# Layer two of a fused attention and two-layer MLP kernel: one operand sum moved from a DMA to VectorE, one summing DMA queued later, and another pair of steps sharing its weight tiles

## The chip, the core and the metric

The kernel runs on one core of a Trainium2 chip. The time is the device time of one launch in microseconds (us). The kernel before took 1100.82 us as the median of three runs (1098.08 to 1101.04). All profiles here are of one execution on the chip. Names of engines: PE is TensorE, ACT is ScalarE, DVE is VectorE, POOL is GpSimd, SP is SyncE.

## The reference, cut to what matters

```python
def reference(q, k, v, tau, ...):              # N = 6016 tokens, C = 256, F1 = 1536, F2 = 2048
    x = attention(q, k, v, tau)                # column norms, softmax over a 256 x 256 score, v @ a
    x = rms_norm(x) * rms_g                    # layer one
    g = x @ w_gate
    x = (silu(g) * (x @ w_val)) @ w_out
    h = x @ w_in                               # layer two, 256 -> 2048 -> 256
    return (h - tanh(h)) @ w_out2
```

Everything is float32. The kernel splits each operand into a high and a low part and multiplies three times (high x high, low x high, high x low) with the faster matmul form, so one "product" below is three matmuls.

## The kernel before, in words

Tokens stand in columns. They are worked through in pairs of blocks of 512 columns (one pair has two blocks of 448). Layer two takes five full pairs and, last, the pair of 448.

In layer two a pair is worked in eight units (`j` = 0 to 7), each 256 of the 2048 hidden rows. Two blocks of hidden rows times two blocks of tokens make a 2 x 2 block product, and `unit` computes it with seven products instead of eight (PSUM banks X, T, Y, Z; the seven weights are S3, A11, A22, A12, S1, S2, S4). In each unit ACT copies bank X to bank Y (`Yh<-Xh`) before PE can go on with `Yh<-T2`; ACT copies T to `m5`; DVE adds Y and m5 into Z and into `s`. Then each of the four results goes through tanh on ACT and a subtraction on DVE: c11, c12, c22, c21.

The output matrix is applied in two ways. Units 6 and 7 use plain products (`second_unit`; weights from `out2_weight`; operands named `uc`). Units 0 to 5, called steps here, use seven products too (`second_seven`, class `Seven`): W11 takes c11, S1 takes c11 + c12, N3 takes c12 + c22, M2 takes c11 + c12 + c22; these four come in a first phase. After step 5 the four accumulator banks are copied away (`turn`, tiles `part`) and combined by four summing DMAs; in a second phase W12 takes c21, S4 takes c22, and W22 takes c11 + c12 + c22 + c21. Every operand is split into high and low by one ACT copy and one DVE subtraction (`split_form`), named by its product: `uW`/`ulW`, `uS`/`ulS`, `uN`/`ulN`, `uM`/`ulM`.

The operand sums are made by DMAs that add into SBUF (`add_by_dma`, L463). They are issued by POOL and follow one another in its queue. A step of before has four of them: c11 += c12, c12 += c22, c11 += c22, c11 += c21. In the trace a step's tiles have these names: step 0 c11 and c22 are `keepwraw`, c21 `keepvh`; step 1 c11 is `keepvh`, c22 and c21 `keepvraw`; step 2 c11 and c22 are `keepvl`, c21 `keeprr`; step 3 `keepwy`, `keepw12h`; step 4 `keepw12l`, `keepw11h`; step 5 `keepw11h`, `keepw11l`. c12 is always `wc`.

SBUF has no room for all output weights. Units 6 and 7 therefore take the place of weights that two steps need only in the first phase (W11, N3, M2, S1): `bring` copies in from DRAM the weights of unit 6 or 7 (`l26p`, `l27p`), and after that unit copies the step's own back (`l20p`, `l21p`). Before, the two steps are 0 and 1 (`SHARED` = 2), tiles `l20h`, `l20l`, `l21h`, `l21l` and two tiles that both print as `l2q`. Each turn is 512 KB per unit. SP issues these DMAs, the loads of the next pair (`y`), and the stores of the results (`outT`).

The order of all instructions is made before the build by a planner (`Graph.run` and `schedule`). It simulates the five queues with fixed costs; PE operations are ranked by a due key, and the output products get their key as "now plus a lag" (`LAG1`, `LAG2`, `LAG7`, `PHASE2`, in ns). Each engine then runs its list strictly in order. A summing DMA is planned to be done at `ADD_SETUP + ADD_TIME + ADD_SLACK` after its issue, and later if another one or an SP transfer is on the wire.

Of the kernel before, what the change touches and what calls it, by code (L numbers as in the profile page):

```python
# [39 lines left out]
PATIENT, HOLD, TOLERANCE = ("ACT", "DVE"), 900.0, 60.0  # L40
DMA_SETUP, DMA_RATE, DMA_TAIL, DMA_ISSUE = 1000, 390.0, 900, 450
DMA_SLACK = 2200
ADD_ISSUE, ADD_SETUP, ADD_TIME, ADD_SLACK = 900, 1440, 1560, 850
STALL, STALL_COST = 40.0, 300.0


# [273 lines left out]
BEHIND = 4  # L320
WARM = 6
MARGIN = 450.0
LAG0, LAG1, LAG2 = 4100.0, 11000.0, 9500.0
SEVEN2, SHARED = 6, 2
LAG7 = dict(W11=3500.0, S1=8750.0, N3=8000.0, M2=9500.0)
PHASE2 = dict(W12=(250.0, 3050.0), S4=(5250.0, 2500.0), W22=(4250.0, 7000.0))
SKEW = 2


# [1 line left out]
def attn_moe_kernel(  # L331
# [129 lines left out]
        return o  # L461

    def add_by_dma(out, in_):  # L463
        g.op("POOL", ADD_ISSUE, lambda: nc.gpsimd.dma_start(  # L464
            out=ap(out), in_=ap(in_), accum_op=ALU.add), [in_, out], [out])

    def prod(out, w, x, n, start, key=None):
# [832 lines left out]
    class Seven(Accumulate):  # L1300

        def __init__(self, forms, group, units, sizes, finish, lag, lag7, home, weight):
            super().__init__(weight, 2 * (units - group), sizes, finish, lag, home)
            self.forms, self.group, self.lag7 = forms, group, lag7
            self.started, self.rest = set(), []

        def at(self, t, m):
            if (t, m) not in self.o:
# [11 lines left out]
                f(at)  # L1320

        def turn(self):
            n = self.sizes[0]
            self.kept = {}
            for t, m in ((0, 0), (1, 0), (0, 1), (1, 1)):
                k = self.kept[t, m] = sq_tile(f"part{t}{m}")
                activation(k[:, :n], self.at(t, m), AF.Copy, n, **(
                    dict(scale=-1.0) if t != m else {}))
                del self.o[t, m]
            self.started = set()  # L1330
            for a, b in (((1, 1), (0, 0)), ((0, 1), (1, 1)), ((1, 1), (1, 0)), ((1, 0), (0, 1))):
                add_by_dma(self.kept[a][:, :n], self.kept[b][:, :n])

        SUMS = {(0, 0): ("add", (0, 0)), (1, 0): ("sub", (1, 1)), (0, 1): ("add", (0, 1)),
                (1, 1): ("sub", (1, 0))}
# [144 lines left out]
    def second_seven(j, x, n, A, keep):  # L1480

        T = dict(c11=keep[0], c12=ut(f"wc12{j}")[:, :n], c22=keep[1], c21=keep[2])
        T = {c: cols(t, n) for c, t in T.items()}

        def form(name, c, t, m):
            A.form(j, name, split_form(f"{name}{j}", T[c], n), t, m)

        def out(c):
            def f(src):
                t = T[c]  # L1490
                activation(t, src, AF.Tanh, n)
                tt("sub", t, src, t, n)
                if c == "c11":
                    form("W11", "c11", 0, 0)
                if c == "c12":
                    add_by_dma(T["c11"], T["c12"])
                    form("S1", "c11", 1, 0)
                if c == "c12":
                    add_by_dma(T["c12"], T["c22"])
                    add_by_dma(T["c11"], T["c22"])  # L1500
                    form("N3", "c12", 0, 1)
                    form("M2", "c11", 1, 1)
                if c == "c21":
                    add_by_dma(T["c11"], T["c21"])
            return f

        def out_sum(Y, m5):
            s = cs(f"s22_{j}")[:, :n]
            add(s, Y, m5, n)
            out("c22")(s)  # L1510

        unit(unit2[j], x, n, f"h{j}", out("c11"), out_sum, out("c12"), out("c21"))

        def second(name, c, t, m):
            return lambda key: A.form(j, name, split_form(f"{name}{j}", T[c], n), t, m, key)

        return dict(W12=second("W12", "c21", 0, 0), S4=second("S4", "c22", 1, 0),
                    W22=second("W22", "c11", 0, 1))
# [173 lines left out]

    forms7 = [{} for _ in range(SEVEN2)]
    plain = []
    split2 = {j: new_dram(f"l2{j}p", [P, 2, 2 * C]) for j in (*range(SHARED), *range(SEVEN2, NU2))}
    shared = {}

    def out_sums(j):
# [8 lines left out]
        for i, name in enumerate(("S4", "M2", "S1")):  # L1707
# [1 line left out]
                s.view(lambda t, x=x, i=i: t[:, (3 * x + i) * P:(3 * x + i + 1) * P],  # L1709
                       k if i == 0 else "one")  # L1710
                for x, k in enumerate("hl"))
        if j < SHARED:
            shared[j] = [(s.view(lambda t: t.rearrange("p (x n) -> p x n", x=2)[:, :, P:], "one"),
                          lambda a: a[:, :, C:], 2)]
            shared[j] += [(out2[j][x].view(lambda t: t[:, 3 * C:], "one"), lambda a, x=x: a[:, x, :C], 1)
# [10 lines left out]

    def out2_weight(f, m):
        k, i = f // 2 - SEVEN2, f % 2
        sums, h, l = (o.buf for o, _, _ in shared[k])
        if i == 0:  # L1730
            at = 3 * C + m * P
            return tuple(x.view(lambda t: t[:, at:at + P], "one") for x in (h, l))
        return tuple(sums.view(lambda t, x=x: t[:, (3 * x + 1 + m) * P:(3 * x + 2 + m) * P], "one")
                     for x in range(2))
# [32 lines left out]
    for p, after in zip(SECOND, [*SECOND[1:], None]):  # L1767
# [9 lines left out]
        for j in range(NU2):  # L1777
            if j < SEVEN2:
                second.append(second_seven(j, x, n, A, keep[3 * j:3 * j + 3]))
                if j < SHARED:  # L1780
                    bring(SEVEN2 + j, j)
                if j + 1 == SEVEN2:
                    A.turn()
                    A.rest = sorted(
                        (g.main + at + i * step, name, i, second[i][name])
                        for name, (at, step) in PHASE2.items() for i in range(SEVEN2))
# [2 lines left out]
                A.flush(float("inf"))  # L1789
            second_unit(j, x, n, A, (after, j) == (None, NU2 - 1))  # L1790
            if after is not None:
                bring(j - SEVEN2, j - SEVEN2)
        for _ in thread:
            pass

# [36 lines left out]
```

## Time and profile before

| what | value |
|---|---|
| median of three runs | 1100.82 us |
| the profiled execution | 1100.79 us, span 1099.0 us |
| PE busy | 1084.1 us (99%) |
| DVE busy | 928.5 us (84%) |
| ACT busy | 740.8 us (67%) |
| POOL busy (issuing DMAs) | 147.3 us (13%) |
| granted TensorE clock | 1.00 in nearly all slices, mean 0.999 |
| layer two | from about 620 us on |

Busy time of PE is the union of matmul intervals that overlap (a 512-column matmul is shown with some 385 ns while the next one starts earlier), so short stalls are better seen in how many matmuls start in a stretch than in the busy share. A gap in front of an instruction, and what ended it, stands in square brackets in the timeline.

### The profile page before, as it was taken

What the parts mean: (1) busy time and instruction counts of PE and PEld (TensorE: products, weight loads), DVE (VectorE), ACT (ScalarE), POOL (GpSimd) and SP (SyncE); (2) the same over time, 40 slices, a digit from 0 to 9 for tenths busy, and PEclk for the clock granted to TensorE, in tenths of its full rate; (3) what the DMA queues carried; (4) which work ended last, traced back from release to release, by engine and by line L of the source; (5) the groups of instructions that cost most, each with busy time, mean ns of one, the idle gap of its engine ahead of it and who ended that gap; (6) DMA issues with size and microseconds to landing.
All of it is one profiled execution on the core that took longest, in us unless ns stands there. A gap on an engine that the chain in (4) does not pass through costs nothing.

```text
span 1099.0 us, 14761 instructions
## 1 busy us (share of the span) xinstructions
PE 1084.1 (99%) x4836; PEld 898.7 (82%) x4836; DVE 928.5 (84%) x1638; ACT 740.8 (67%) x1338; POOL 147.3 (13%) x174
## 2 busy tenths in 40 slices
PE   9999999999999999999999999999999999999998
PEld 8889988888888888888888888878877878778897
DVE  6999897986888799688867989979978979878787
ACT  7686476565566656656665879669668668677675
POOL 0000000000000000000000043143142142152151
PEclk9999999999999999999999999999999999999999
DMA  9953121114212221322343396597586596595493
GB/s 353 379 195 112 59 72 39 59 39 136 68 47 62 93 86 54 105 87 68 112 135 92 112 216 126 119 183 128 129 171 128 129 169 129 126 167 102 119 176 81
DMA packets 83437, 136.33 MB, mean 124 GB/s; under 512 B 9632, under 2 KB 35104, under 8 KB 83360
## 3 DMA queue, kind: packets, MB, share of 16 engines
q1 hardware_dynamic: 58736, 91.87, 25.2%
q0 software_dynamic: 24192, 43.13, 23.2%
q8 instruction: 38, 0.62, 0.2%
q10 hardware_dynamic: 432, 0.38, 0.1%
q14 instruction: 39, 0.32, 0.1%
HBM read 66.72 MB, written 25.45 MB: 84 GB/s over the span
## 4 chain that ended last, share of the span: by engine, by line
PE 81%; DMA 7%; DVE 4%; issue 4%; ACT 2%; POOL 1%; SPq 0%; DVEq 0%; ACTq 0%; POOLq 0%
PE acc L474 32%; PE Yv L474 6%; PE Yh L474 6%; PE Yg L474 6%; PE Xg L474 4%; PE Xv L474 4%; PE Xh L474 4%; PE S L482 3%; PE v L474 2%; PE g L474 2%; PE Zv L474 2%; PE Zg L474 2%; PE Tg L474 2%; PE Tv L474 2%; PE Zh L474 2%
## 5 line engine op out<-in xcount | busy, mean ns | idle before, releaser
L432 ACT ACTIVATE uc<-tc 128x512 fp32r<-128x512 f32 x120 | 75.2, 631 | 84.1 <-PE acc L474 71.9
L464 POOL DMA_DIRECT2D keepwraw<-wc x6 | 5.4, 892 | 685.7 <-DVE ulW L451 685.7
L451 DVE TENSOR_TENSOR ulc<-tc,uc 128x512 fp32r<-128x512 f32 x120 | 81.5, 683 | 18.2 <-ACT uc L432 15.6
L447 DVE TENSOR_TENSOR Zh<-Yh,m5h 128x512 f32<-128x512 f32 (+1 forms) x48 | 32.9, 685 | 14.6 <-PE Yh L474 11.3
L474 PE MATMUL acc<-uS,l2q 128*128 128x512 f32 (+1 forms) x144 | 43.8, 386 | 0.0
L482 PE MATMUL S<-q,k 128*128 128x256 f32 x188 | 42.4, 385 | 0.8 <-DMA k<-k_in 0.8
L447 DVE TENSOR_TENSOR Zv<-Yv,m5v 128x512 f32<-128x512 f32 x30 | 20.9, 698 | 25.7 <-PE Yv L474 19.3
L482 PEld LDWEIGHTS S<-q,k 128*128 128x128 f32 x188 | 35.8, 193 | 6.1 <-issue 1.1
L432 ACT ACTIVATE uN<-wc 128x512 fp32r<-128x512 f32 (+1 forms) x36 | 22.4, 622 | 23.8 <-DMA wc<-keepw12h 9.4
L447 DVE TENSOR_TENSOR s<-Yh,m5h 128x512 f32<-128x512 f32 (+1 forms) x48 | 32.4, 674 | 5.5 <-PE Yh L474 4.8
L451 DVE TENSOR_TENSOR ulN<-wc,uN 128x512 fp32r<-128x512 f32 (+1 forms) x36 | 24.4, 678 | 14.7 <-ACT uN L432 13.7
L447 DVE TENSOR_TENSOR acc<-acc,sq 128x512 f32<-128x512 f32 (+1 forms) x46 | 29.4, 677 | 8.4 <-ACT sq L432 7.7
L474 PE MATMUL Yh<-T2h,l2s 128*128 128x512 f32 (+1 forms) x96 | 30.4, 398 | 5.8 <-ACT Yh L432 5.6
L432 ACT ACTIVATE Yh<-Xh 128x512 f32<-128x512 f32 (+1 forms) x48 | 27.6, 575 | 11.8 <-DVE wc L447 8.5
L432 ACT ACTIVATE wc<-Zh 128x512 f32<-128x512 f32 (+1 forms) x48 | 27.7, 577 | 11.5 <-PE Zh L474 11.5
L447 DVE TENSOR_TENSOR wc<-Zh,wc 128x512 f32<-128x512 f32 (+1 forms) x48 | 32.3, 673 | 2.9 <-ACT wc L432 2.9
L432 ACT ACTIVATE m5h<-Th 128x512 f32<-128x512 f32 (+1 forms) x48 | 28.1, 585 | 9.3 <-PE Th L474 8.6
L451 DVE TENSOR_TENSOR ulc<-wc,uc 128x512 fp32r<-128x512 f32 (+1 forms) x48 | 31.9, 674 | 1.8 <-ACT uc L432 1.2
L432 ACT ACTIVATE uc<-wc 128x512 fp32r<-128x512 f32 (+1 forms) x48 | 29.4, 620 | 4.2 <-PE acc L474 3.7
L432 ACT ACTIVATE Yg<-Xg 128x512 f32<-128x512 f32 x30 | 17.5, 583 | 20.6 <-PE Xg L474 9.0
L474 PEld LDWEIGHTS acc<-uS,l2q 128*128 128x128 f32 x144 | 27.0, 188 | 5.0
L474 PE MATMUL acc<-uc,w10l 128*128 128x512 f32 x80 | 31.1, 389 | 0.0
(1107 smaller groups left out, 3939.4 us busy)
## 6 DMA issues: line engine op xcount, KB each, us to landing
vraw<-vT_in SPq DMA_DIRECT2D x11, 512.0 KB, 4.2
y<-r SPq DMA_DIRECT2D x22, 256.0 KB, 2.7
part<-part POOLq DMA_DIRECT2D x20, 256.0 KB, 3.4
outT<-part SPq DMA_DIRECT2D x20, 256.0 KB, 4.4
q<-q_in SPq DMA_DIRECT2D x8, 512.0 KB, 9.7
k<-k_in SPq DMA_DIRECT2D x8, 512.0 KB, 9.7
raw<-w_in_in SPq DMA_DIRECT2D x8, 512.0 KB, 4.0
l<-y SPq DMA_DIRECT2D x16, 256.0 KB, 2.2
```

The lines of the kernel that those rows point to most:

```text
L432: nc.scalar.activation(out=ap(out), in_=ap(in_), func=func, **{x: ap(a) for x, a in kw.items()})
L447: return dve(lambda: f(out=ap(out), in0=ap(a), in1=ap(b)), n, 2, [a, b], [out])
L451: lambda: nc.vector.tensor_sub(out=ap(out), in0=ap(in_), in1=f32(ap(hi))), n, 2,
L464: g.op("POOL", ADD_ISSUE, lambda: nc.gpsimd.dma_start(out=ap(out), in_=ap(in_), accum_op=ALU.add), [in_, out], [out])
L474: nc.tensor.matmul(o, ap(a), ap(b), start=start and i == 0, stop=i == 2, skip_group_check=True)
L482: lambda: nc.tensor.matmul(ap(out), ap(a), ap(b), start=start, stop=stop, **kw),
```

## The change

Per step, c11 += c12 is a DVE addition now; the other three sums stay DMAs. The last of them, c11 += c21, is put on a list (`sums`) and issued behind the next step's c11 += c22 (`add_sums`, with an explicit order against it); what is left on the list goes out at `turn`. The tiles shared with units 6 and 7 are those of steps 4 and 5 instead of 0 and 1: the weights of units 6 and 7 are brought in after step 5 has been written down, and brought back after units 6 and 7. The lags, the start and step of the second-phase products, and the planner's `ADD_SLACK` have new values; these set the order alone.

```diff
-ADD_ISSUE, ADD_SETUP, ADD_TIME, ADD_SLACK = 900, 1440, 1560, 850
+ADD_ISSUE, ADD_SETUP, ADD_TIME, ADD_SLACK = 900, 1440, 1560, 1200
-LAG0, LAG1, LAG2 = 4100.0, 11000.0, 9500.0
+LAG0, LAG1, LAG2 = 4100.0, 9250.0, 7750.0
-LAG7 = dict(W11=3500.0, S1=8750.0, N3=8000.0, M2=9500.0)
-PHASE2 = dict(W12=(250.0, 3050.0), S4=(5250.0, 2500.0), W22=(4250.0, 7000.0))
+LAG7 = dict(W11=6250.0, S1=6000.0, N3=8000.0, M2=9750.0)
+PHASE2 = dict(W12=(250.0, 2300.0), S4=(4000.0, 2500.0), W22=(4500.0, 2250.0))
...
         def turn(self):
+            self.add_sums()
...
+        def add_sums(self, last=None):
+            for out, in_ in self.sums:
+                o = add_by_dma(out, in_)
+                if last is not None:
+                    o.preds.setdefault(last, None)
+            self.sums = []
...
                 if c == "c12":
-                    add_by_dma(T["c11"], T["c12"])
+                    add(T["c11"], T["c11"], T["c12"], n)
+                    add_by_dma(T["c12"], T["c22"])
                     form("S1", "c11", 1, 0)
-                if c == "c12":
-                    add_by_dma(T["c12"], T["c22"])
-                    add_by_dma(T["c11"], T["c22"])
+                    last = add_by_dma(T["c11"], T["c22"])
+                    A.add_sums(last)
                     form("N3", "c12", 0, 1)
                     form("M2", "c11", 1, 1)
                 if c == "c21":
-                    add_by_dma(T["c11"], T["c21"])
+                    A.sums.append((T["c11"], T["c21"]))
...
-        if j < SHARED:
+        if j >= SEVEN2 - SHARED:
...
             if j < SEVEN2:
                 second.append(second_seven(j, x, n, A, keep[3 * j:3 * j + 3]))
-                if j < SHARED:
-                    bring(SEVEN2 + j, j)
                 if j + 1 == SEVEN2:
                     A.turn()
+                    for k in range(SHARED):
+                        bring(SEVEN2 + k, SEVEN2 - SHARED + k)
...
             if after is not None:
-                bring(j - SEVEN2, j - SEVEN2)
+                bring(j - SHARED, j - SHARED)
```

On ACT, the first place is around step 4 of the third pair. In the order of before, `uS<-keepvl` is the S1 operand of step 2, `Yh<-Xh` the copy of step 4 that PE waits for, `uM` the M2 operand of step 1 and `uN<-wc` (second from the end) the N3 operand of step 2:

```order
L432 ACTIVATE wc_7956<-Zh_7922 128x512
L432 ACTIVATE keepw12h_7946<-Yh_7892 128x512
L432 ACTIVATE uS_7973<-keepvl_7851 128x512
L432 ACTIVATE Yh_7978<-Xh_7958 128x512
L432 ACTIVATE m5h_7987<-Th_7969 128x512
L432 ACTIVATE uM_7992<-keepvh_7673 128x512
L432 ACTIVATE keepw12l_8005<-Xh_7958 128x512
L432 ACTIVATE uN_8012<-wc_7871 128x512
L432 ACTIVATE uW_8019<-keepw12l_8005 128x512
```

The same place in the order of after, where `uN<-wc` is the N3 operand of step 2, `uM` the M2 operand of step 2 and `uS` the S1 operand of step 3:

```order
L432 ACTIVATE wc_7959<-Zh_7936 128x512
L432 ACTIVATE keepw12h_7964<-s_3_7953 128x512
L432 ACTIVATE uW_7967<-keepwy_7941 128x512
L432 ACTIVATE uN_7973<-wc_7892 128x512
L432 ACTIVATE keepw12h_7964<-Yh_7913 128x512
L432 ACTIVATE Yh_7987<-Xh_7977 128x512
L432 ACTIVATE uM_7994<-keepvl_7866 128x512
L432 ACTIVATE m5h_8000<-Th_7990 128x512
L432 ACTIVATE uS_8008<-keepwy_7941 128x512
```

The S1 operand no longer stands right ahead of the copy to Y, and each step of after repeats the same ten places.

On SP, the second place is the start of the fourth pair. Before, `part` are the results of the third pair, `l20`, `l21` and `l2q` the shared tiles, `l20p`, `l21p` the steps' own weights and `l26p`, `l27p` those of units 6 and 7:

```order
L458 DMA l2q_5648<-l21p 128x2x256
L458 DMA outT<-part_8295 128x512
L458 DMA outT<-part_8260 128x512
L458 DMA l21h<-l21p 128x256
L458 DMA l21l<-l21p 128x256
L458 DMA outT<-part_8158 128x512
L458 DMA outT<-part_8271 128x512
L458 DMA l20h<-l26p 128x256
L458 DMA l20l<-l26p 128x256
L458 DMA l2q_5575<-l26p 128x2x256
L458 DMA l21h<-l27p 128x256
L458 DMA l21l<-l27p 128x256
```

After, the same stores stand between the transfers that bring back the weights of steps 4 and 5, and then come the loads for units 6 and 7 of the fourth pair and the first load of the pair after the next one:

```order
L458 DMA l2q5_5982<-l25p_138 128x2x256
L458 DMA outT<-part11_8316 128x512
L458 DMA outT<-part10_8255 128x512
L458 DMA l25h_5999<-l25p_138 128x256
L458 DMA l25l_6024<-l25p_138 128x256
L458 DMA outT<-part00_8196 128x512
L458 DMA outT<-part01_8286 128x512
L458 DMA l24h_5836<-l26p_139 128x256
L458 DMA l24l_5849<-l26p_139 128x256
L458 DMA l2q4_5815<-l26p_139 128x2x256
L458 DMA y000_9054<-y0_94 128x384
```

The list is the same length, but the loads of `l26p` stand behind products of step 4 now and not behind products of step 0.

## Rows read from the trace of the kernel before

**Rows 1.** Stretches: length, busy (x instructions) of PE, PEld, DVE, ACT, POOL, clock, DMA.

```profile
200.00:600.00 400.00, 400.00 (x1762) 329.86 (x1761) 326.82 (x589) 244.44 (x435) 0.00 (x0) 1.00 0.26 82
625.47:704.31 78.84, 78.83 (x346) 64.36 (x345) 71.63 (x117) 62.06 (x115) 24.58 (x29) 1.00 0.73 150
704.31:784.49 80.18, 78.73 (x342) 63.33 (x342) 69.32 (x113) 58.87 (x109) 24.35 (x28) 1.00 0.71 145
784.49:866.20 81.71, 79.71 (x344) 63.57 (x343) 70.31 (x114) 59.19 (x109) 24.42 (x28) 1.00 0.69 142
866.20:946.83 80.63, 78.30 (x344) 63.93 (x343) 70.17 (x115) 59.00 (x109) 24.48 (x28) 1.00 0.69 140
946.83:1027.06 80.23, 78.62 (x343) 63.41 (x342) 65.69 (x106) 57.47 (x106) 24.44 (x28) 1.00 0.66 131
```

**Rows 2.** Waits of PE from 620 us on: total us, times, longest.

```profile
PE Yh L474 <- ACT Yh L432: 5.6, 8, 2.0
PE acc L474 <- ACT uN L432: 1.0, 2, 0.8
PE acc L474 <- ACT uM L432: 1.0, 1, 1.0
```

**Rows 3.** Timeline of the fourth pair: start, us, engine, instruction, idle before it.

```profile
882.63 1.52 POOL L464 DMA_DIRECT2D keepvl<-wc  x1
...
889.69 0.63 ACT L432 ACTIVATE uS<-keepvl 128x512 fp32r<-128x512 f32 x1 [1.60 <-DMA keepvl<-wc]
890.00 0.86 POOL L464 DMA_DIRECT2D wc<-keepvl  x1 [3.46 <-DMA keepvl<-wc]
890.22 0.58 ACT L432 ACTIVATE Yh<-Xh 128x512 f32<-128x512 f32 x1
890.35 0.69 DVE L451 TENSOR_TENSOR ulS<-keepvl,uS 128x512 fp32r<-128x512 f32 x1 [1.15 <-ACT uS L432]
...
890.85 0.50 PE L474 MATMUL Yh<-T2h,l2s 128*128 128x512 f32 x1 [2.00 <-ACT Yh L432]
```

**Rows 4.** Waits of ACT from 620 us on: total us, times, longest.

```profile
ACT uN L432 <- DMA wc<-keepw12h: 9.4, 6, 2.5
ACT uN L432 <- DMA wc<-keepvraw: 7.7, 4, 3.1
ACT uM L432 <- DMA keepwraw<-keepwraw: 5.6, 6, 1.9
ACT uS L432 <- DMA keepw11h<-wc: 4.1, 4, 1.8
ACT uS L432 <- DMA keepvl<-wc: 2.2, 2, 1.6
```

**Rows 5.** DMA issues, 882 to 883 us: KB each, us to landing.

```profile
keepvl<-wc POOLq DMA_DIRECT2D x1, 256.0 KB, 7.0
```

**Rows 6.** DMA issues, 997 to 1001 us.

```profile
keepw11h<-keepw11l POOLq DMA_DIRECT2D x1, 256.0 KB, 3.3
```

**Rows 7.** DMA issues, 868 to 880 us.

```profile
outT<-part SPq DMA_DIRECT2D x4, 256.0 KB, 4.6
...
keepvh<-wc POOLq DMA_DIRECT2D x1, 256.0 KB, 5.5
...
l20h<-l26p SPq DMA_DIRECT2D x1, 128.0 KB, 4.1
```

**Rows 8.** Timeline of DVE, three instructions that follow without a wait.

```profile
871.51 0.68 DVE L447 TENSOR_TENSOR part<-part,acc 128x512 f32<-128x512 f32 x1
872.11 0.68 DVE L447 TENSOR_TENSOR keepvraw<-Yh,keepvraw 128x512 f32<-128x512 f32 x1
872.71 0.68 DVE L451 TENSOR_TENSOR ulS<-keepwraw,uS 128x512 fp32r<-128x512 f32 x1
```

**Rows 9.** Costliest groups on the page: busy us, mean ns of one.

```profile
L451 DVE TENSOR_TENSOR ulc<-tc,uc 128x512 fp32r<-128x512 f32 x120 | 81.5, 683 | 18.2 <-ACT uc L432 15.6
```

**Rows 10.** Busy time of a stretch inside the first pair, columns as in rows 1.

```profile
650.00:700.00 50.00, 49.99 (x219) 40.66 (x218) 46.71 (x76) 41.66 (x77) 14.83 (x17) 1.00 0.70 136
```

More of the change, by code (lines that the diff above doesn't have):

```diff
@@ L463, in add_by_dma @@
     def add_by_dma(out, in_):
-        g.op("POOL", ADD_ISSUE, lambda: nc.gpsimd.dma_start(
+        return g.op("POOL", ADD_ISSUE, lambda: nc.gpsimd.dma_start(
             out=ap(out), in_=ap(in_), accum_op=ALU.add), [in_, out], [out])
@@ L1304, in __init__ @@
             self.forms, self.group, self.lag7 = forms, group, lag7
-            self.started, self.rest = set(), []
+            self.started, self.rest, self.sums = set(), [], []
         def at(self, t, m):
@@ L1694, in attn_moe_kernel @@
     plain = []
-    split2 = {j: new_dram(f"l2{j}p", [P, 2, 2 * C]) for j in (*range(SHARED), *range(SEVEN2, NU2))}
+    split2 = {j: new_dram(f"l2{j}p", [P, 2, 2 * C]) for j in range(SEVEN2 - SHARED, NU2)}
     shared = {}
@@ L1728, in out2_weight @@
         k, i = f // 2 - SEVEN2, f % 2
-        sums, h, l = (o.buf for o, _, _ in shared[k])
+        sums, h, l = (o.buf for o, _, _ in shared[SEVEN2 - SHARED + k])
         if i == 0:
```

## The prediction, made before the run

> **What bounds the kernel now.** I read the busy table first: PE 99%, the other engines far below. Since matmul intervals overlap in this trace, 99% does not mean that nothing is lost, so I next counted matmuls by stretch [rows 1]. In 200 to 600 us, in layer one, 1761 of them start in 400 us: 0.2271 us each, with no stall. A full pair of layer two has 8 units x 7 products x 3, plus 6 steps x 7 x 3, plus 2 units x 4 results x 2 x 3 = 342 matmuls, or 77.7 us at that pace. The five full pairs, cut at each pair's first summing DMA, take 78.84, 80.18, 81.71, 80.63 and 80.23 us: 1.1, 2.5, 4.0, 3.0 and 2.5 us too long, 13.2 us in all. The reader is to see that the DMA share in these rows is about 0.70 against 0.26 in layer one, and that the first pair, where DVE is densest, loses least (part of its 1.1 is work, since its stretch holds 2 to 4 matmuls more than the others).
>
> What PE waits for is in the waits: chiefly the copy of bank X to Y on ACT, 5.6 us in 8 waits, and then split operands that ACT makes [rows 2]. Such a gap understates the loss, since a matmul is shown some 0.16 us longer (0.39 against 0.23) than the spacing of starts; the counting above holds both. Why ACT is late is seen in the longest of the eight [rows 3]: ACT stands at `uS<-keepvl` until the DMA c11 += c12 of step 2 lands, 1.60 us; the copy to Y is the next in its queue, and PE has been idle 2.00 us when it comes. That DMA, issued at 882.63, took 7.0 us to land [rows 5]; one of the same size late in a pair took 3.3 [rows 6]. At the start of a pair four stores, the weights of step 1 going back and the weights of unit 6 coming in run beside the sums, and one such sum takes 5.5 us [rows 7]. So the bound is PE, and what is lost in layer two is ACT's queue held up by summing DMAs. ACT waits for them in three kinds of places: `uN`, `uM` and `uS` [rows 4].
>
> **The change part by part.** The matmuls stay the same in number and shape, so PE's floor stays, and only the excess can move: 13.2 us in the full pairs, and in the last pair about 1.2 (its one wait of 1.0 for `uM` [rows 2] and 0.2 for the spacing). Together 14.4 us; a gain beyond that is excluded.
>
> First sum on DVE. It takes 36 of 144 summing DMAs of layer two away, and ACT's waits at `uS` with them (4.1 and 2.2 us are the two largest [rows 4]); what follows in POOL's queue goes out one place, some 0.9 us, earlier. It adds 36 additions on DVE. Three DVE instructions in a row start 0.60 us apart although one is shown with 0.68 [rows 8]; so 36 x 0.60 = 21.6 us, 3.6 per pair. By the code DVE has 113 instructions of this size in a full pair now (48 in the units, 50 low parts, 4 results, 11 for the next pair's operands) and 119 then: 71.4 us of 77.7, or 92%. What hides it is that DVE was not the bound at 46.71 of 50 us, 93%, while PE was busy for 49.99 [rows 10]. If that cover is gone, the price is that of the slower rival below. Per step, ACT's new order gives the two remaining sums this much time: c12's difference, the c22 difference, two low parts, c21's and the sum are six DVE places, 3.6 us, before c12 += c22 may go; `uN` stands one step (33 matmuls, 7.5 us) and two ACT places (1.2 us) after c12's tanh. So 5.1 us are left for an add that lands in 3.3 us undisturbed [rows 6], and in 5.5 to 7.0 at a disturbed start [rows 5, 7]: nothing lost inside a pair, up to 1.9 us per pair at its start if the company stays as it is.
>
> Last sum behind the next step's. c11 += c21 is read in the second phase alone, so nobody waits for it. It now waits for `ulM` of its step, which is done by then, and behind it in POOL's queue stands only the next step's c12 += c22, one step later. I cost it at 0; from 0 to 0.9 us (one place) if it is late.
>
> Shared tiles of steps 4 and 5. Bringing in the weights of unit 6 used to wait for the N3 and M2 products of step 0, and so fell into the first 12 us of a pair, beside the stores [rows 7]. Now it waits for products of step 4 and falls behind step 5, where the four `part` sums run; in the new order 21 products, 63 matmuls or 14 us, lie between the last M2 of step 4 and the first product that reads the incoming weights, against 4 us that such a load takes [rows 7]. The weights that go back are not wanted for four steps, 30 us. What is late next is the rest: four stores and 512 KB going back still stand at the start of a pair. So the company there shrinks by the 1 MB for units 6 and 7, and by one sum in four. I cost the move at 0 and its gain as part of the excess.
>
> Lags, `PHASE2` and `ADD_SLACK`. They change the order of PE everywhere, layer one too, where PE is busy 400.00 of 400 us [rows 1]; nothing can be won there, and a stall of a few tenths lost: I take 0, with 0.5 us as the bad end. The second phase is pressed together: from unit 7 to step 1 of the next pair the new order has 63 DVE instructions to 174 matmuls, 37.8 us to 39.5, or 96%. That is above anything the rows show; 0 to 1 us per pair, and I take 0.3.
>
> How much of 14.4 us stays? The nearest rows are the first pair's. It has the same four sums, but no stores of an earlier pair and no weights going back at its start, and it loses 1.1 us or less. I take 0.4 for a pair's start and 0.3 for the second phase, 0.7 per pair, 4.2 in six. The sum: 14.4 - 4.2 = 10.2 us, and 1100.79 (the profiled execution, whose span is 1099.0) - 10.2 = 1090.6 us. That execution lies at the median of the runs, 1100.82, so the sum stands against the median too.
>
> A rule of the Trainium skill speaks against the first part: SBUF — State Buffer, Who interferes with whom, says that a VectorE instruction with both inputs in SBUF contends with a GpSimd instruction that reads SBUF, and whichever comes second is blocked to the end of the first. The added sums have both inputs in SBUF. If POOL's issuing counted as such, each of the 36 could cost DVE up to the 0.86 us of an issue, 31 us in all, and the kernel would be slower. In the trace a POOL issue runs from 890.00 to 890.86, and `ulS`, with both inputs in SBUF, starts beside it at 890.35 and takes 0.69 us as elsewhere [rows 3]; so by the row it costs nothing, and I go by the row.
>
> **The rivals.** (a) Only the waits at `uS` go, and those at `uN` and `uM`, still DMA sums, eat the rest. For it: the largest waits of ACT are those, 9.4 and 7.7 us [rows 4]. Against it: they come late because of the queue of four and the company, and both get smaller. Price: take the listed `uS` waits, 6.3 us of 29, as the share of 14.4 that goes: 3.1 us, so 1097.7 us.
>
> (b) No change: what the sums no longer hold up is held up by stores at a pair's start and by DVE in the second phase. 1.9 + 1 us per pair over six is 17.4 us, more than is lost now; at the mean of today's loss, 14.4 : 6 = 2.4 per pair, the time stays 1100.8.
>
> (c) Slower: DVE becomes the bound. If its instructions cannot be set 0.60 us apart, since each waits for a fresh result, and cost the 0.683 of one [rows 9], a pair takes 119 x 0.683 = 81.3 us; five of them 406.4 against 401.6, and the time is 1105.6 us. It decides from 77.7 : 119 = 0.653 us per instruction. For it: 92% in a strict order, with a step's chain ACT, DVE, DMA, ACT. Against it: DVE at 93% in [rows 10] and the spacing in [rows 8].
>
> (d) The change doesn't do what it says, that is, the new order puts `uN` or `uM` right ahead of the copy to Y. In the order of before it was `uS`; in the new order `uN` stands two places ahead and c21's tanh between. It ends as (a).
>
> **How the numbers follow.** The forecast, 1090.6 us, has 0.64, with its own range from 1086.5 (nearly all of 14.4 us goes) to 1094.8 (half of the pairs' excess stays). Between that and (a), 1094.8 to 1097.5, 0.16; (a) beyond that and (b) 0.12; (c) 0.08. A measurement of this kernel can tell about 0.3%, 3.3 us, from no change: below 1097.5 is faster, 0.80; up to 1104 the same, 0.12; above, 0.08. The range from 1086.5 to 1098 leaves out some 0.03 below and 0.17 above.
>
> **What would show it.** In the profile after: matmuls per pair still 342, and pairs of about 78.4 us; no wait of ACT at `uS` for a DMA; PE's waits for the copy to Y down from 5.6 to about 2 us; DVE with 36 more additions and a share near 87% of the span; the issue of 36 fewer DMAs on POOL. (a) would show `uN` and `uM` waits as long as now; (c) would show PE waiting for the addition into Z and ACT for DVE's differences in all steps, not at the starts alone. The forecast is wrong if pairs stay above 80 us, and the step that failed is then named by who holds ACT in front of the copy to Y.

## The result, and the profile after

The changed kernel takes 1085.61 us, the median of 4 runs (1085.30 to 1086.95); the kernel before, run beside it, 1100.93 (1098.08 to 1101.49). The ratio is 0.9868, with a 95% interval from 0.9849 to 0.9887: 15.3 us less. The forecast of 1090.6 us had the sign and the mechanism, but the time lies 0.9 us below the low end of the range. Medians and ratios, here and below, are over fast executions: a slow one of f1_two (3882.87 us) and one of f2_three (1206.79 us) are left out.

The busy table of the profile after, engine by engine, as busy time, share of the span and instructions:

```profile
span 1084.1 us, 14708 instructions
...
PE 1077.9 (99%) x4836; PEld 900.9 (83%) x4836; DVE 945.6 (87%) x1674; ACT 739.6 (68%) x1338; POOL 116.3 (11%) x138
```

VectorE's share is the 87% that was forecast, and PE's 99% still tells nothing. The stretches between the first summing DMAs of the pairs do; these rows answer to [rows 1], with the same columns:

```profile
200.00:600.00 400.00, 400.00 (x1759) 328.53 (x1758) 323.28 (x590) 242.95 (x434) 0.00 (x0) 1.00 0.25 79
626.20:704.02 77.82, 77.82 (x344) 63.97 (x343) 75.41 (x125) 62.85 (x117) 19.39 (x22) 1.00 0.62 132
704.02:781.82 77.80, 77.80 (x345) 64.27 (x344) 73.55 (x120) 59.34 (x110) 19.26 (x23) 1.00 0.61 129
781.82:858.92 77.10, 77.10 (x342) 63.85 (x341) 73.17 (x119) 58.48 (x110) 19.22 (x22) 1.00 0.61 130
858.92:936.59 77.67, 77.67 (x344) 64.23 (x343) 73.13 (x121) 59.15 (x110) 19.27 (x23) 1.00 0.59 125
936.59:1013.39 76.80, 76.80 (x344) 64.11 (x343) 69.23 (x114) 57.60 (x107) 19.27 (x23) 1.00 0.57 117
```

The five pairs take 77.4 us on average, against 80.3 before and a floor of 77.7: nothing is left to win in them. (The third stretch holds two matmuls fewer than a pair, and 34 matmuls of the fifth are already narrower ones of the last pair, hence the two under the floor.) In all of them PE is busy from end to end. All that PE waits for in the whole run, as total, times and longest (answers to [rows 2]):

```profile
PE nrm L482 <- DVE mean L529: 1.1, 1, 1.1
PE Yh L474 <- DVE Zh L447: 0.5, 1, 0.5
```

The first wait is at the very start of the span (1.1 us) and is in both kernels. Of layer two only the second is left, at 1022.9 us in the last pair. Among the waits of ACT from 610 us on, one kind alone is still for a transfer (answers to [rows 4]):

```profile
ACT uM L432 <- DMA keepwraw<-keepwraw: 3.4, 5, 1.3
```

So that losses can be compared between kernels, I counted them in each trace in one way: from 600 us on, the distance between the starts of successive matmuls, less the 0.227 us that 512 columns take at PE's pace (and less for narrower ones), summed where it is over 0.03 us. By this count layer two loses 15.6 us before and 1.2 us after, 14.4 us less. The count leaves out what is lost in distances under its limit. From the start of the same matmul at 602 us (the 2701st) to that of the last one, before takes 492.5 us and after 477.3, 15.2 us less. The spans differ by 14.9 us: at the 201st matmul after is 0.4 us ahead, and the rest of layer one takes it 0.7 us longer. In the first 50 us one wait of before is absent after:

```profile
PE S L482 <- DMA k<-k_in: 0.8, 1, 0.8
```

What the sums now look like inside a pair is seen in POOL's and ACT's timeline of the fourth (start, length, engine, instruction):

```profile
874.77 0.88 POOL L464 DMA_DIRECT2D wc<-keepvl  x1 [3.80 <-DVE keepvl L447]
...
876.58 0.87 POOL L464 DMA_DIRECT2D keepvl<-keepvl  x1 [0.92 <-DVE ulS L451]
...
878.98 0.62 ACT L432 ACTIVATE uN<-wc 128x512 fp32r<-128x512 f32 x1
...
880.66 0.62 ACT L432 ACTIVATE uM<-keepvl 128x512 fp32r<-128x512 f32 x1
```

`wc<-keepvl` is c12 += c22; it landed in 3.28 us, at 878.05, and ACT's split `uN` starts 0.93 us later without a wait. The other steps inside pairs look alike, some 7.4 us apart; in the five full pairs `uN` follows the landing by 0.8 to 1.3 us in 22 of 25 of them. At the start of a pair the sums have company; the issues from 855 to 875 us, with KB and us to landing (answers to [rows 5 to 7]):

```profile
outT<-part SPq DMA_DIRECT2D x4, 256.0 KB, 4.4
wc<-keepwraw POOLq DMA_DIRECT2D x1, 256.0 KB, 3.3
...
keepwraw<-keepwraw POOLq DMA_DIRECT2D x1, 256.0 KB, 5.5
wc<-keepvraw POOLq DMA_DIRECT2D x1, 256.0 KB, 3.3
```

The stores are still there, but c12 += c22 of step 0 (`wc<-keepwraw`) lands in 3.3 us, and in 3.3 to 3.6 in every pair; before, it took 4.1 to 5.1 in the pairs that follow another. Only c11 += c22 of step 0 lands late, and ACT waits 0.47 to 0.55 us for it in four pairs without any loss to PE. In the last pair ACT's wait is 1.34, and PE loses the 0.5 us shown above (0.8 by the spacing).

### The profile page after: what moved, and what is told of

It reads as the page before. It is cut to its first block, busy times and chain, and to the rows that moved or that the text cites. A ratio compares the mean times of both kernels' runs of the same rounds, so it can differ in the third digit from the quotient of the medians.

```text
span 1084.1 us, 14708 instructions
## 1 busy us (share of the span) xinstructions
PE 1077.9 (99%) x4836; PEld 900.9 (83%) x4836; DVE 945.6 (87%) x1674; ACT 739.6 (68%) x1338; POOL 116.3 (11%) x138
## 4 chain that ended last, share of the span: by engine, by line
PE 96%; ACT 2%; DVE 1%; DMA 0%; issue 0%; POOL 0%; DVEq 0%; ACTq 0%; POOLq 0%
PE acc L474 39%; PE Yh L474 9%; PE Xh L474 6%; PE Yv L474 6%; PE Yg L474 6%; PE Xg L474 4%; PE Xv L474 4%; PE S L482 4%; PE Zh L474 3%; PE Th L474 3%; PE v L474 2%; PE g L474 2%; PE Zg L474 2%; PE Zv L474 2%; PE Tg L474 2%; PE Tv L474 2%
## 5 line engine op out<-in xcount | busy, mean ns | idle before, releaser
L451 DVE TENSOR_TENSOR ulc<-tc,uc 128x512 fp32r<-128x512 f32 x120 | 80.3, 684 | 1.8 <-ACT uc L432 1.6
L464 POOL DMA_DIRECT2D wc<-keepwraw x6 | 5.4, 894 | 683.6 <-DVE keepwraw L447 624.9
L447 DVE TENSOR_TENSOR wc<-Zh,wc 128x512 f32<-128x512 f32 (+1 forms) x48 | 32.6, 679 | 12.8 <-ACT wc L432 12.3
L432 ACT ACTIVATE tc<-Zg 128x512 f32<-128x512 f32 x30 | 18.0, 599 | 31.2 <-PE Zg L474 27.7
L432 ACT ACTIVATE tc<-Xg 128x512 f32<-128x512 f32 x30 | 17.9, 597 | 21.8 <-PE Xg L474 21.6
L474 PE MATMUL acc<-uc,w11h 128*128 128x512 f32 x80 | 31.1, 389 | 0.0
L474 PE MATMUL acc<-ulc,w10h 128*128 128x512 f32 x80 | 31.1, 389 | 0.0
L474 PE MATMUL acc<-uc,w10h 128*128 128x512 f32 x80 | 31.1, 389 | 0.0
```

What stands on the lines that cost most here:

```text
L432: nc.scalar.activation(out=ap(out), in_=ap(in_), func=func, **{x: ap(a) for x, a in kw.items()})
L447: return dve(lambda: f(out=ap(out), in0=ap(a), in1=ap(b)), n, 2, [a, b], [out])
L451: lambda: nc.vector.tensor_sub(out=ap(out), in0=ap(in_), in1=f32(ap(hi))), n, 2,
L464: return g.op("POOL", ADD_ISSUE, lambda: nc.gpsimd.dma_start(out=ap(out), in_=ap(in_), accum_op=ALU.add), [in_, out], [out])
L474: nc.tensor.matmul(o, ap(a), ap(b), start=start and i == 0, stop=i == 2, skip_group_check=True)
```

## The experiments

The theory: ScalarE's queue stood behind a chain of landings, and VectorE's sum takes one landing out of it. Rival 1: the company of the transfers was the cause, whoever waits. Rival 2: the new order did it. All results in one table; "loss" is layer two's by the count above. The losses are those of the profiled executions; f1_two's is read from the trace of f1_again, the same kernel, and the profiled execution of e2_late is its slowest, 1104.48 us. In every kernel but the two with added small transfers the span less this loss is 1083 to 1086 us, so the loss accounts for the time to some 3 us.

| kernel | median us | ratio to before, 95% | loss, us |
|---|---|---|---|
| before | 1099.3 to 1101.1 | 1 | 15.6 |
| changed | 1085.61 | 0.9868 [0.9849, 0.9887] | 1.2 |
| a1_sum | 1091.47 | 0.9924 [0.9907, 0.9941] | 5.5 |
| a2_share | 1099.17 | 0.9984 [0.9972, 0.9996] | 13.7 |
| a3_numbers | 1109.38 | 1.0086 [1.0069, 1.0104] | 22.9 |
| a4_defer | 1105.12 | 1.0048 [1.0034, 1.0061] | 21.7 |
| b1_no_sum | 1100.39 | 0.9992 [0.9982, 1.0003] | 14.2 |
| b2_no_share | 1089.24 | 0.9892 [0.9876, 0.9908] | 3.0 |
| b3_old_numbers | 1091.21 | 0.9912 [0.9893, 0.9932] | 4.4 |
| b4_no_defer | 1088.26 | 0.9882 [0.9867, 0.9898] | 3.6 |
| d2_before_order_dve | 1090.19 | 0.9910 [0.9895, 0.9924] | 4.8 |
| d1_after_order_dma | 1149.21 | 1.0443 [1.0422, 1.0464] | 62.7 |
| e2_late | 1097.49 | 0.9988 [0.9971, 1.0005] | 12.3 |
| e3_late | 1151.68 | 1.0458 [1.0433, 1.0483] | 58.3 |
| f1_two | 1093.09 | 0.9934 [0.9916, 0.9953] | 10.3 (f1_again) |
| f2_three | 1108.87 | 1.0079 [1.0054, 1.0104] | 22.1 |

Not all of this loss is waiting. In six traces PE's granted clock falls in layer two from 1.00 to 0.50, the 1.2 GHz level, beside waits of PE of 0.8 to 6.2 us, and matmuls of 512 columns then start 0.43 us apart. The loss in these stretches is 1.6 us in a3_numbers, 3.0 in a4_defer, 4.7 in d1, 1.5 in e2_late, 9.3 in e3_late and 1.7 in f1_again. The traces of the other kernels have no such stretch while matmuls run, so the comparisons of before, after, a1_sum, a2_share, b1 to b4, d2 and f2_three do not rest on it. Two stretches of e3_late, columns as above:

```profile
822.00:825.00 3.00, 3.00 (x15) 2.45 (x14) 2.84 (x5) 1.64 (x3) 1.79 (x2) 1.00 1.07 113
829.50:832.50 3.00, 3.00 (x8) 2.32 (x8) 2.44 (x5) 1.66 (x3) 1.28 (x2) 0.50 0.30 52
```

### One part at a time, added to the kernel before

a1_sum:

```diff
-                    add_by_dma(T["c11"], T["c12"])
+                    add(T["c11"], T["c11"], T["c12"], n)
```

> The kernel before with one part of the change: c11+=c12 of each step runs on VectorE, all else as before (the order is planned anew around it). Theory (ScalarE's queue stood behind the landing of this sum, its wait at uS): the uS waits for a transfer go, and with them most of the loss that VectorE's one sum can reach, 7 to 11 of the 15.3 us: 1090 to 1094 us. Rival 1 (the transfers themselves are slow when five sums follow each other, whoever waits; the deferral and the move of the stores cure that): 1097 to 1101 us, the waits only move to uN and uM. Rival 2 (the new lags and slack set the order and do nearly all of it): within 2 us of before.

1091.47 us, as the theory had it: 9 us of the gain. No wait at `uS` for a transfer is left. The longest that remain are those of `uN` and `uM` of step 1 on the two other sums, 3.8 and 3.6 us in all.

a2_share (the sharing steps are 4 and 5; the weights come back behind step 5):

```diff
-        if j < SHARED:
+        if j >= SEVEN2 - SHARED:
...
-                if j < SHARED:
-                    bring(SEVEN2 + j, j)
                 if j + 1 == SEVEN2:
                     A.turn()
+                    for k in range(SHARED):
+                        bring(SEVEN2 + k, SEVEN2 - SHARED + k)
```

> The kernel before with one part of the change: the two steps that share tiles with units 6 and 7 are steps 4 and 5, so that their weights are brought back later; sums, lags and slack as before. Theory: the stores of units 0 and 1 leave the first two steps of a pair, sums there land sooner, but ScalarE still waits at uS: 0 to 2 us less, 1099 to 1101 us. Rival 1 (company of transfers is the cause): 5 us less or more, 1096 us or under.

1099.17 us, 1 to 2 us less: rival 1 falls as far as these transfers go, for less company alone changes little.

a3_numbers:

```diff
-LAG0, LAG1, LAG2 = 4100.0, 11000.0, 9500.0
+LAG0, LAG1, LAG2 = 4100.0, 9250.0, 7750.0
```

(and with it `ADD_SLACK`, `LAG7` and `PHASE2` as in the change)

> The kernel before with one part of the change: the new lags of the second layer's work (LAG1, LAG2, LAG7, PHASE2) and ADD_SLACK 1200 instead of 850; every sum still a transfer. Theory: the planner leaves more time between a sum and its split, which cuts some of the waits at uM and uN but pushes work together elsewhere: 1097 to 1102 us. Rival 2 (the numbers do nearly all of it): 1086 to 1090 us.

1109.38 us, 9 us slower than before, and worse than either expected. Rival 2 falls as far as it says that the numbers do it alone: with the sums still in line as transfers, the new numbers only add loss.

a4_defer:

```diff
-                    add_by_dma(T["c11"], T["c22"])
+                    last = add_by_dma(T["c11"], T["c22"])
+                    A.add_sums(last)
...
-                    add_by_dma(T["c11"], T["c21"])
+                    A.sums.append((T["c11"], T["c21"]))
```

> The kernel before with one part of the change: c11+=c21 of a step is issued behind the next step's sums. Theory: nobody waits for this sum within its step, and the next step's first sum starts without its company; the wait at uS shrinks by some tenths of a us in five of six steps but stays: 1 to 4 us less, 1097 to 1100 us. Rival 1 (company of transfers is the cause): 1090 to 1095 us.

1105.12 us: slower than before by 5 us, a miss for both. PE's waits of layer two in this trace are of the old kind and longer than before (5.6 in [rows 2]), and 3.0 of the 21.7 us of loss are the lower clock behind the longest of them:

```profile
PE Yh L474 <- ACT Yh L432: 6.5, 7, 2.7
```

### One part at a time, taken from the changed kernel

b1_no_sum:

```diff
-                    add(T["c11"], T["c11"], T["c12"], n)
+                    add_by_dma(T["c11"], T["c12"])
```

> The changed kernel without one of its parts: c11+=c12 is a transfer again, the rest (deferral, sharing with steps 4 and 5, new numbers) stays. Theory (ScalarE behind the landing of this sum): waits at uS for a transfer come back, 6 to 11 us of the gain are lost: 1092 to 1097 us. Rival 1 (company of transfers): 0 to 3 us lost, 1086 to 1089 us. Rival 2 (the numbers): within 1 us of the changed kernel.

1100.39 us: all of the gain is gone, more than the theory had. ACT's waits at `uS` for this sum are back, the two largest of its waits for transfers being

```profile
ACT uS L432 <- DMA keepwraw<-wc: 8.9, 5, 2.4
ACT uM L432 <- DMA keepwraw<-keepwraw: 5.4, 4, 2.2
```

So the three other parts together are worth nothing without the sum (ratio 0.9992), though with it they are worth 5.9 us (a1_sum to the changed kernel).

b2_no_share:

```diff
-        if j >= SEVEN2 - SHARED:
+        if j < SHARED:
```

(and the weights brought back at steps 0 and 1, as before)

> The changed kernel without one of its parts: steps 0 and 1 share their tiles with units 6 and 7 again, whose weights are brought back there. Theory: c12+=c22 lands later in the first two steps of a pair (5 to 7 us instead of 3.3 to 3.5), over the 5.1 us that a step has for it; this is where the 0.4 us per pair were expected that the changed kernel does not show: 1086.5 to 1089 us. Rival: within 0.5 us of the changed kernel, since the sum on VectorE left room enough.

1089.24 us, 3.6 more than the changed kernel. Not by the expected way: at the pair starts c12 += c22 of step 0 lands in 3.1 to 3.7 us, not in 5 to 7. In the fourth pair c11 += c22 is late and ACT waits 1.06 us for it, where the changed kernel's wait is 0.47, and PE loses 0.8 us there. The rest of the loss lies scattered in small pieces. The ratio's interval overlaps that of the changed kernel.

b3_old_numbers:

```diff
-LAG0, LAG1, LAG2 = 4100.0, 9250.0, 7750.0
+LAG0, LAG1, LAG2 = 4100.0, 11000.0, 9500.0
```

(and the three others back too)

> The changed kernel without one of its parts: the lags and the slack of the kernel before. Theory: each step's splits come due earlier than their sums land in some steps, and the second phase is less even: 1086.5 to 1090 us. Rival 2 (the numbers do nearly all of it): 1096 to 1101 us.

1091.21 us, just above the expected stretch. Waits of ACT for sums, and of PE for the copy to Y behind them, come back in some steps:

```profile
PE Yh L474 <- ACT Yh L432: 1.3, 2, 0.9
```

b4_no_defer:

```diff
-                    last = add_by_dma(T["c11"], T["c22"])
-                    A.add_sums(last)
+                    add_by_dma(T["c11"], T["c22"])
...
-                    A.sums.append((T["c11"], T["c21"]))
+                    add_by_dma(T["c11"], T["c21"])
```

> The changed kernel without one of its parts: c11+=c21 follows at once in its own step. Theory: it lies ahead of no split of its own step, and meets the next step's c12+=c22 only at its end: 1085.5 to 1088 us. Rival 1 (company of transfers): 1090 to 1095 us.

1088.26 us, 2.7 more; here too the ratios' intervals overlap, so the worth of this part and of the sharing is the least certain. Most of its loss lies in the last pair and the second phase behind it, where c11 += c22 of step 0 takes 6.2 us to land and ACT waits 2.5 us for it.

In all eight kernels the order is planned anew, so they show what a part is worth with its own order, not the part alone. The small differences of b2 to b4 lie in layer two only in part by the count (1.9, 3.3 and 2.4 us more than after); between the same two matmuls as above the three take 3.5, 3.6 and 2.6 us more. Of b3's remainder 1.1 us lies behind the last matmul.

### The sum alone, with the order held

d2_before_order_dve (planned as before, another instruction issued):

```diff
-                    add_by_dma(T["c11"], T["c12"])
+                    g.op("POOL", ADD_ISSUE, lambda: nc.vector.tensor_add(
+                        out=ap(T["c11"]), in0=ap(T["c11"]), in1=ap(T["c12"])),
+                        [T["c12"], T["c11"]], [T["c11"]])
```

> The kernel before in its own order, but the instruction issued in the place of each transfer c11+=c12 is VectorE's addition. Theory (ScalarE behind a chain of transfers): this alone shortens the chain by a landing (3.3 to 7.0 us instead of 0.6), the waits at uS for a transfer go, those at uN and uM shrink, PE's excess in layer two falls from 15.6 to 3 to 8 us: 1088 to 1094 us. Rival (the order that is planned around the part does it): less than 4 us gained, 1097 to 1101 us.

1090.19 us. In the very order of before (apart from the 36 instructions the traces have the same lists on all engines), replacing 36 transfers by additions takes 10.9 of the 15.6 us away. PE's wait for the copy to Y falls from 5.6 us in 8 waits to one, while ACT still waits for the two other sums:

```profile
PE Yh L474 <- ACT Yh L432: 0.8, 1, 0.8
```

```profile
ACT uN L432 <- DMA wc<-keepw12h: 5.7, 5, 1.7
ACT uM L432 <- DMA keepwraw<-keepwraw: 3.5, 5, 1.4
```

The line itself is seen in POOL's waits. Before, c12 += c22 is held up by the landing of c11 += c12 in 25 of the 36 steps, 57 us in all; the largest row is

```profile
POOL wc L464 <- DMA keepvh<-wc: 17.5, 5, 5.7
```

In d2 POOL has no such wait, and ACT's waits for transfers fall from 8.3 to 0 us at `uS`, from 22.6 to 7.0 at `uN` and from 8.4 to 4.7 at `uM`. It was not less company that did it: c12 += c22 lands no sooner in d2 (median 4.3 us) than before (4.1). So rival 1 falls here too, and rival 2 with the order.

d1_after_order_dma (planned as the changed kernel, a transfer issued):

```diff
-                    add(T["c11"], T["c11"], T["c12"], n)
+                    dve(lambda: nc.gpsimd.dma_start(out=ap(T["c11"]), in_=ap(T["c12"]), accum_op=ALU.add),
+                        n, 2, [T["c11"], T["c12"]], [T["c11"]])
```

> The changed kernel in its own order, but c11+=c12 is a transfer issued from GpSimd in the place of VectorE's addition. Theory: c12+=c22 must wait until it has read c12, so a step has two landings in a row where there is room for one: some 3.6 us (0.9 issue and 3.3 landing less 0.6) later against 0.9 us between landing and uN, so up to 2.7 us in each of 36 steps, less what ScalarE has of room: 1110 to 1180 us. Rival (room is ample in the new order): within 8 us of the changed kernel, 1086 to 1094 us.

1149.21 us, 64 more than the changed kernel, 1.8 per step: its order has no room for a second landing in line. ACT waits at `uS` in 32 of the 36 steps. The late split holds VectorE at `ulS` in all 36 (63.0 us), and PE waits for `s` behind it, 43.5 us in 35 waits; 4.7 us of the loss are the lower clock. The largest line of ACT:

```profile
ACT uS L432 <- DMA keepvh<-wc: 18.3, 6, 3.5
```

### How much room a landing has

e2_late, and e3_late with LATE = 3:

```diff
+    LATE = 2
+    tiny = [dram.tile([P, 2], F32, tag=f"late{i}", name=f"late{i}") for i in range(LATE + 1)]
+    def late_add(out, in_):
+        def emit():
+            for i in range(LATE):
+                nc.gpsimd.dma_start(out=tiny[i], in_=mean32.t)
+            nc.gpsimd.dma_start(out=ap(out), in_=ap(in_), accum_op=ALU.add)
...
-                    add_by_dma(T["c12"], T["c22"])
+                    late_add(T["c12"], T["c22"])
```

> The changed kernel, its order kept, with two transfers of 1 KB issued on GpSimd ahead of each c12+=c22: it and c11+=c22 go out and land some 1.7 us later (two issues of 0.86), c12+=c22 about 5.0 us after it could go. By the prediction's room of 5.1 us: nothing is lost, 1085 to 1088 us. By the room seen in the trace of the changed kernel (uN starts 0.93 us behind the landing, 4.2 us in all) and no further room on ScalarE: 0.8 us in each of 36 steps, 28 us, 1114 us.

> The same with three such transfers: c12+=c22 lands about 5.9 us after it could go. By the prediction's room of 5.1 us: 0.8 us in each of 36 steps, 28 us, 1114 us. By a room of 4.2 us: 1.7 us in each, 60 us, 1146 us. If ScalarE's own room behind the wait covers it (the changed kernel waits up to 1.3 us at uM and PE loses nothing): under 5 us, below 1091 us.

1097.49 us (from 1095.53 to 1104.48) and 1151.68 us. Against the changed kernel, 6 and 9 us of the two profiled spans are lost ahead of layer two: in the first 20 us PE waits 3.3 and 5.6 us for `k`, and the granted clock is 0.50 for part of the time. Why stays open. Both expectations rest on a delay that did not happen. The small transfers have no data to wait for, so POOL issues them right behind the sums of the step before, long ahead of their own sum. At the start of the third pair of e2_late:

```profile
792.78 0.88 POOL L464 DMA_DIRECT2D keepwraw<-keepwraw  x1 [0.66 <-DVE ulS L451]
793.36 1.44 POOL L473 DMA_DIRECT2D late<-mean  x2
799.52 0.90 POOL L474 DMA_DIRECT2D wc<-keepvraw  x1 [4.72 <-DVE keepvh L447]
```

They act as company. From 790 to 800 us in e2_late:

```profile
keepwraw<-keepwraw POOLq DMA_DIRECT2D x1, 256.0 KB, 6.8
...
late<-mean POOLq DMA_DIRECT2D x2, 1.0 KB, 7.9
```

That is still a dose. In the changed kernel and these two, whose planned order is one, a wait of ACT for a sum can be set beside PE's loss (spacing) from 3 us before its end to 6 us after. At `uM` at the pair starts, waits of 0.46 to 0.55 us cost nothing in five cases, 1.8 to 2.0 us cost 0.8 to 0.9, and 2.3 cost 1.1: ACT has 0.5 to 1.2 us to spare there. At `uN` inside pairs it has less. Waits of 0.64 and 1.96 us cost 0.26 and 1.58, and in e3_late two of 3.0 cost 2.8 and 4.3, the latter with 1.6 us of lower clock in it: 0.2 to 0.4 us to spare in these four, at most 0.8 in the others, beside the 0.93 us by which `uN` follows an undisturbed landing. So c12 += c22 has 3.3 + 0.9 + 0.2 to 0.8, which makes 4.4 to 5.0 us in all. The prediction's 5.1 us is a little too much, and it had put all of it ahead of `uN`, where the trace has 4.2. Why three small transfers hurt inside pairs where two do little (c12 += c22 lands in 4.3 to 7.7 us in four steps between 743 and 776 us of e3_late) stays open.

### How far VectorE carries

f1_two, and f2_three with the second line too:

```diff
-                    add_by_dma(T["c12"], T["c22"])
+                    add(T["c12"], T["c12"], T["c22"], n)
...
-                    last = add_by_dma(T["c11"], T["c22"])
-                    A.add_sums(last)
+                    add(T["c11"], T["c11"], T["c22"], n)
+                    A.add_sums()
```

> The changed kernel with c12+=c22 on VectorE as well (the order is planned anew): 125 VectorE instructions of 512 columns in a full pair, 75.0 us of 77.4 at 0.60 us each. Theory: the uN wait is gone for good and VectorE, at 97%, still keeps up for most of the pair: 1085 to 1092 us. Rival (VectorE becomes the bound, at 0.653 us per instruction or more): 125 x 0.653 = 81.6 us per pair, 4.2 x 6 = 25 us more, 1110 us or over.

> The changed kernel with c12+=c22 and c11+=c22 on VectorE: 131 instructions in a full pair, 78.6 us at 0.60 us each against PE's 77.4. Theory: VectorE is the bound by 1.2 us per pair and PE starts to wait for its results: 7 us more at least, 1092 to 1100 us. Rival (0.653 us per instruction): 85.5 us per pair, 49 us more, 1134 us. If below 1089 us, VectorE's instructions can be set closer than 0.60 us apart.

> f1_two once more, for its profile: 1093 us. Theory (VectorE at its limit): full pairs of 78.4 to 79.2 us, VectorE without idle time in the steps, TensorE waiting for VectorE's results (Zh, s), ScalarE for no sum. Rival (landings): ScalarE waits at uM for c11+=c22 by 0.9 us and more in most steps and TensorE waits for the copy to Y.

f1_two took 1093.09 us, 7.5 more than the changed kernel, f1_again 1096.27. Its trace agrees with neither side whole. PE's one kind of wait in layer two is for VectorE; but ACT's only waits for a transfer are five at pair starts and one of 0.2 us, and the longest of these, 3.6 us for a sum that took 8.0 us to land, stands beside 4.6 of the 10.3 us lost, 1.7 of them in the lower clock:

```profile
PE Yh L474 <- DVE Zh L447: 3.7, 3, 2.7
```

```profile
ACT uM L432 <- DMA keepwraw<-keepwraw: 7.8, 5, 3.6
```

f2_three took 1108.87 us, 23 more than the changed kernel, three times what 0.60 us per place allows for. Two of its pairs, columns as above:

```profile
718.63:800.74 82.11, 79.45 (x341) 62.87 (x340) 81.10 (x133) 60.63 (x109) 8.67 (x11) 1.00 0.35 85
800.74:881.88 81.14, 79.40 (x343) 63.57 (x343) 80.30 (x132) 60.38 (x109) 8.66 (x10) 1.00 0.36 85
```

VectorE is busy 99% of them, and its instructions start 0.62 us apart on average, not 0.60. Its timeline shows longer places:

```profile
724.51 0.69 DVE L447 TENSOR_TENSOR keepvl<-s,keepvl 128x512 f32<-128x512 f32 x1
725.11 0.69 DVE L447 TENSOR_TENSOR keepvl<-keepvl,wc 128x512 f32<-128x512 f32 x1
725.84 0.69 DVE L447 TENSOR_TENSOR wc<-wc,keepvl 128x512 f32<-128x512 f32 x1
726.56 0.69 DVE L451 TENSOR_TENSOR ulS<-keepvl,uS 128x512 fp32r<-128x512 f32 x1
```

The third instruction, c12 += c22, follows the second by 0.73 us instead of 0.60: it overwrites c12, which the second still reads, and starts as that one ends. The fourth starts as ACT's `uS` ends. Over four pairs the places are 12.1 us longer than 0.60 each; 2.4 us of this lie in front of c12 += c22, 3.8 in front of the addition into Z (`Zh`), and 3.0 in front of `ulS` and `ulN`, which need ACT's split. PE then waits for `Zh` 20 times, 12.0 us in all. Here VectorE is the bound, its places drawn out by what stands between its own and ACT's instructions.

## Why the prediction was wrong, point by point

- The bound: right. PE's floor stayed (the five pairs average 77.4 us against 77.7), and layer two's excess moved. The cause was right too: with the order held, taking the landing of c11 += c12 out of ACT's queue is worth 10.9 us of loss (d2), and putting it in costs 64 us (d1).
- The ceiling, "14.4 us; a gain beyond that is excluded": mis-sized. By spacing the loss before was 15.6 us, 13.7 in the five pairs and 2.0 in the last one (13.2 and 1.2 were taken), and the profiled execution of before held a 0.8 us wait for k at its start besides.
- **The step that failed**: how much of the excess stays, "0.4 for a pair's start and 0.3 for the second phase, 0.7 per pair, 4.2 in six". The trace after has 1.2 us in all, 0.2 per pair. Of the 5.0 us between forecast and median this term is 3.0, the ceiling 1.2, what the count does not hold 0.5, and 0.3 is between executions.
- Why it failed: deferral, shared tiles and lags were costed at 0, one by one. The forecast is, to within 1 us, what the sum alone gives (1090.19 and 1091.47 us), and d2's remaining loss of 4.8 us is close to the 4.2 that were kept. That closeness is luck: the prediction put its 4.2 at the pairs' starts and in the second phase, and in d2 only 1.1 us lie in the first 12 us of the pairs, while 2.1 lie 12 to 18 us behind the first sum. The other three parts take that remainder: with the sum in place, leaving out one of them costs 2.7, 3.6 or 5.6 us. Alone they give +4.8, -1.2 and +9.0 us. The parts are not additive, and no term of the sum stood for that. How each does it, apart from the order planned with it, is not shown.
- The pair's start: 5.5 to 7.0 us of landing were carried over from [rows 5, 7], where three sums of a step stand in line beside the stores. These are landings of c11 += c12 in steps 1 and 2; c12 += c22 of step 0, for which they were used, took 3.6 to 5.1 before and takes 3.3 to 3.6 after. This is so with the sharing undone too (b2, 3.1 to 3.7), so it was not the returning weights that made it late. With one of the two others it is 3.1 to 4.6 us (d2, fewer sums in the order of before) and 3.3 to 4.9 (d1, four sums in the order of after), so each brings a part of it.
- The high end of the range, 1094.8, is said to be half of the pairs' excess; half of 13.2 gives 1094.2. It does not bear on the outcome.
- The second phase at 96% of VectorE: 0.3 us per pair were taken and under 0.1 us was lost there in the full pairs. The 0.60 us per place held: after, too, instructions that wait for nothing start 0.604 us apart on average in four pairs.
- Rival (a) fell: the waits at `uN` vanished with those at `uS`. With the sum alone they fell from 22.6 to 7.0 us (d2), because they came late through the same chain; the rest went with the other parts. Rival (b) fell. Rival (c), 0.683 us per instruction, fell at 119 instructions a pair; f2_three shows what it would have looked like, at 131 and 0.62 us. Its point of decision, 0.653 us, is reached nowhere.
- The rule weighed in the prediction (the Trainium skill, SBUF — State Buffer, Who interferes with whom) stays without effect after: `ulS`, with both inputs in SBUF, starts at 868.14 beside a POOL issue that runs from 867.41 to 868.28 and takes 0.68 us. The 36 additions take 0.68 us at the median and 0.69 at most.

The row on POOL and the row on VectorE behind the last point:

```profile
867.41 0.87 POOL L464 DMA_DIRECT2D wc<-keepvraw  x1 [5.86 <-DVE keepvh L447]
...
868.14 0.68 DVE L451 TENSOR_TENSOR ulS<-keepvh,uS 128x512 fp32r<-128x512 f32 x1
```

Not tried: a delay of one sum by a known time with nothing beside it, and the deferral or the sharing with the order held. What each of those two does apart from its order stays open.

## What to carry to other kernels

When several transfers stand in line in front of one in-order engine, price the line, not its waits one by one: moving the first link to an engine with free places took the waits behind the later links away as well. Do not price the parts of a joint change at 0 because each is idle alone: a part that loosens nothing in the old order can pay once another has made the room, and the reverse (new lags without the sum: 9 us slower). And an engine's free places end a little before the arithmetic says, since an instruction that waits for the one just ahead of it, or for another engine's, takes a longer place (0.62 us on average in f2_three, not 0.60).

## What was not expected of the hardware

- An addition on VectorE that overwrites what the one just ahead reads starts 0.72 to 0.73 us behind it, others 0.60 (f2_three). The Trainium skill (VectorE: DVE Perf Modes, The DRAIN you can't avoid) reports a chain of copies that took as long with a semaphore after each as with one after the last; here the wait costs 0.12 to 0.13 us, and the measurement decides.
- Transfers of 1 KB issued from GpSimd took 3.0 to 12.3 us to land (e2_late, e3_late), and beside them sums of 256 KB took up to 14.9 us (`keepwraw<-keepvh` at 646.68 us of e3_late) instead of 3.3 alone.
- PE's granted clock fell to 0.50 beside waits of PE of a few us, and stayed there for a while after the work had come back (six traces, 1.5 to 9.3 us of loss), so a wait can cost more than its length.
